# Reordering the head of a Strassen attention-and-MLP kernel: load order of x and w_in, one clamp on VectorE, score order, one transpose group moved

## The chip, the cores and the metric

One core of a Trainium2 chip. The metric is the device time of one execution in microseconds, the median of several runs. The engines are TensorE (PE, with its weight loads PEld), VectorE (DVE), ScalarE (ACT), GpSimd (POOL) and SyncE (SP), which here only issues DMAs.

## The reference

```python
# x (8, 8, 512, 64), state (8, 8, 32, 64), w_in (512, 2048), w_out (2048, 512)
def _attn_ref(x, state):
    scores = scale * np.matmul(x, state.transpose(0, 1, 3, 2))
    a = softmax(scores)                       # exp(s - max) / (sum + 1e-9)
    xread = np.matmul(a, state)
    scores2 = scale * np.matmul(state, x.transpose(0, 1, 3, 2))
    a2 = softmax(scores2)
    sread = np.matmul(a2, x)
    return np.concatenate([xread, sread], axis=2)

def _moe_ref(x, w_in, w_out):                 # x: attention's output as 4352 rows of 512
    h = x @ w_in
    g = h * (1.0 / (1.0 + np.exp(-1.702 * h)))
    return g @ w_out
```
In the kernel w_in and w_out arrive as float64 (two 32-bit words a value) and are turned into float32 on the chip. `softmax` is written out in the original.

## The kernel before, in words

Eight batches go one after the other through attention, the up product with w_in, a gelu, and the down product with w_out. The order of all instructions is written out by hand (`tc.manual_schedule()`): each engine works through its own queue in the order of the program text. The two matrices are multiplied together with the attention first: instead of `(a @ state) @ w_in`, a small matrix M = state @ w_in is made for each quarter of w_in (`att_M`), and the up product is `a @ M`. Down products, and the up products from batch 2 on, use Strassen's scheme.

What matters here is the head, before the first up product (`up_x(0, 0, ...)`), in which batches 0 and 1 go through attention while the first quarter of w_in is still arriving.

**Loads.** `load_weights(n)` issues the loads of the weight pieces up to piece n (512 KB each: 128 rows of w_in, 512 columns, two words a value; pieces 0 to 3 are the first quarter of w_in, 4 to 7 the second, w_out begins at 16). `load_x(b)` issues x of batch b: four loads of 256 KB for batch 0, two of 512 KB for batch 1. All are issued by SP in this order, eight semaphores in turn: pieces 0 and 1, x of batch 0, piece 2, x of batch 1, pieces 3 to 7.

**A weight piece.** On VectorE `mask(i)` (L221) takes the exponent bits; a clamp moves it to float32's range, in `round_a`: two ACTIVATEs on ScalarE (L232, L233), or for pieces 18 and 19 two tensor_scalars on VectorE (L229, L230). `fraction(i)` (L239), `sign(i)` (L245) and the two steps of `round_b` (L258, L264) on VectorE give the value. `powers_to(n)` does mask and clamp up to piece n; `piece(fill)` finishes the next piece, with `fill()` between its last two steps; `round_to(n)` finishes pieces up to n.

**Attention of a batch in the head.** `two_states` and `xT_part` transpose states and x on TensorE (L330, L356), ScalarE copies the results out of PSUM (L334, L357). `att_scores` multiplies them (L444): 16 matmuls, each on a quarter of the array's columns (j) and a half of its rows (i). `score_copies` copies the scores to SBUF on ScalarE (L363), `scores_back` transposes them again on TensorE (L372). `head_max` (L379) and `head_sub` (L386) on VectorE, `head_exp` (L390) on ScalarE, `head_sum` (L402 to L405) and `head_scale` (L413) on VectorE make the softmax; `head_back` transposes it on TensorE (L422, copied by L423 on ScalarE). `att_M` is L430 (copied by `M_copies`, L566), `up_x` runs L655.

**Order in the head.** For batch 0: states, x, scores, and then batch 1's states and x woven with batch 0's softmax. In the kernel before, `scores_back(1, i, ...)` stands ahead of `att_M(0, 0)` and `head_back(0, g)`; `head_max(1, i, ...)` comes on VectorE right behind `head_scale(0)`; `up_x(0, 0)`, `up_x(0, 1)` and `up_x(0, 2)` follow, and then `head_back(1, g)`.

**The second place.** In the down products of batch 0 (loop over `i` in `range(HF)`, L1539), at i = 0, an early up product of batch 1 (`up_x(1, f_early, ...)`), `att_srT`, the sums of w_out (`pair_sums`) and the next two pieces (`round_to`) stand between the products P2 and P6.

Of the kernel before, what the change touches and what calls it, by code (L numbers as in the profile page):

```python
# [20 lines left out]
def kernel(  # L21
# [124 lines left out]
        for g in range(NG):  # L146
            nc.sync.dma_start(stn[b][:, g], st_v[b, g])

    def load_x(b):
        t = sums[:, 0] if b == 1 else xpool.tile([P, SCH, H, D], FP32, tag="xn", name=f"xn_{b}").rearrange("p c h d -> p (c h d)")  # L150
        xn[b] = t.rearrange("p (h c d) -> p h c d", h=H, c=SCH)
        n = NPR if b else NG
        for i in range(H // n):
            h = slice(n * i, n * (i + 1))
            nc.sync.dma_start(xn[b][:, h].rearrange("p h c d -> p h (c d)"), x_four[b, :, h])

    def load_x_squares(b):
        xsq[b] = xpool.tile([P, NPR, S], FP32, tag="xn", name=f"xsq_{b}")
# [57 lines left out]
    def mask(i):  # L216

        _, hi = words(i)
        sc = low[:, 2 + i % (AHEAD + 1)].bitcast(I32)
        power[i] = sc  # L220
        nc.vector.tensor_scalar(sc, hi, 0x7FF00000, None, ALU.bitwise_and)  # L221

    def round_a(i):

        if i not in power:
            mask(i)
        sc = power[i]
        if i in (NFC * NPR + 2, NFC * NPR + 3):
            nc.vector.tensor_scalar(sc, sc, most, least, ALU.min, ALU.max)  # L229
            nc.vector.tensor_scalar(sc, sc, -least, 8.0, ALU.add, ALU.mult)  # L230
            return
        nc.scalar.activation(out=sc.bitcast(FP32), in_=sc, func=AF.Relu, bias=edge[0], scale=-8.0)  # L232
        nc.scalar.activation(out=sc, in_=sc.bitcast(FP32), func=AF.Relu, bias=edge[1], scale=-1.0)  # L233

    def fraction(i):

        key = PIECES[i]
        dst = w_in[key[1]][:, key[2]] if key[0] == "i" else w_out[:, key[1]]
        nc.vector.tensor_scalar(dst.bitcast(I32), words(i)[1], 0xFFFFF, 0x100000, ALU.bitwise_and, ALU.bitwise_or)  # L239
        begun[i] = dst  # L240
# [32 lines left out]
    def load_weights(upto):  # L273
        while done["load"] < min(upto, len(PIECES)):
            load_weight(done["load"])
            done["load"] += 1

    def powers_to(n):
        while done["a"] < min(n, len(PIECES)):
            load_weights(done["a"] + 1)  # L280
            round_a(done["a"])
            done["a"] += 1
# [15 lines left out]
    def piece(fill):  # L298

        i = done["b"]  # L300
        powers_to(i + 1)
        round_b(i, i + 1, False, fill)
        done["b"] += 1
        refill()
# [20 lines left out]
    def two_states(b, banks):  # L325

        A[b]["turn"] = banks
        A[b]["two"] = [apool.tile([P, P], FP32, tag=f"two{i}", name=f"two{i}_{b}", bufs=2) for i in range(2)]
        for ps, t in zip(banks, two):
            nc.tensor.transpose(ps, t[:, b].rearrange("p u d -> p (u d)"), ident)  # L330

    def state_copies(b):
        for t, ps in zip(A[b]["two"], A[b]["turn"]):
            nc.scalar.copy(t, ps)  # L334
# [10 lines left out]
    def xT_part(b, j, bank=None):  # L345

        if j == 0:
            A[b]["xT"] = apool.tile([P, H, 2, P], FP32, tag="xT", name=f"xT_{b}")
        h = slice(NG * j, NG * (j + 1))
        if bank is None:  # L350
            ps = att_ps([P, NG, 2, P], f"xT_{b}_{j}")
        else:
            ps = bank.rearrange("p (g i q) -> p g i q", g=NG, i=2)
        for g in range(NG):
            for i in range(2):
                nc.tensor.transpose(ps[:, g, i], x_pair(b, NG * j + g, i), ident)  # L356
        nc.scalar.copy(A[b]["xT"][:, h], ps)  # L357
# [8 lines left out]
    def scores_back(b, i, bank):  # L366

        ps = bank.rearrange("p (k g m) -> p k g m", k=2, g=NG)
        for k in range(2):
            for g in range(NG):  # L370
                o = P * (2 * g + k)
                nc.tensor.transpose(ps[:, k, g], A[b]["s"][i][:, o : o + P], ident)  # L372

    def head_max(b, i, banks):
        a = A[b]
        if i == 0:
            a["e1"] = apool.tile([P, SCH, NG, NPR, Ns], FP32, tag="e1", name=f"e1_{b}")
            a["mx"] = apool.tile([P, NG, NB], FP32, tag="mx", name=f"mx_{b}")
        nc.vector.reduce_max(out=a["mx"][:, i], in_=banks[i].rearrange("p (k n) -> p k n", n=Ns), axis=AX.X)  # L379
# [8 lines left out]
    def head_exp(b):  # L388
        t = A[b]["e1"]
        nc.scalar.activation(out=t, in_=t, func=AF.Exp, scale=scale)  # L390
# [41 lines left out]
    def att_scores(b):  # L432
        a = A[b]
        a["s"] = bank_o[:NG] if b < 2 else bank_o[NG:]
        if b > 1:
            by_state(b, a["s"], lambda rows, j: a["xT"][rows, j])
            return

        for g in range(NG):
            for j in range(NPR):  # L440
                st = slice(Ns * j, Ns * (j + 1))
                for i in range(2):
                    rows = slice(D * i, D * (i + 1))
                    nc.tensor.matmul(  # L444
                        a["s"][i][st, 2 * P * g : 2 * P * (g + 1)], state_of(b, NG * j + g, i),
                        a["xT"][rows, NG * j + g], start=True, stop=True,
                    )
# [846 lines left out]

    load_two_states()
    load_weights(2)
    load_x(0)
    load_weights(3)
    load_x(1)
    load_weights(2 * NPR)  # L1300
    nc.scalar.activation(out=one, in_=one, func=AF.Exp)
    keep_warm(14)
    powers_to(1)
    fraction(0)
    powers_to(2)
    piece(lambda: fraction(1))
    held, apart = bank_o[NG:], [psH.tile([P, FC], FP32, tag="h", name=f"apart_{i}") for i in range(2)]
    two_states(0, [bank_o[i][:, :P] for i in range(2)])
    state_copies(0)
    keep_warm(3, held[0])  # L1310
    for j in range(NPR):
        xT_part(0, j, apart[j - 2] if j > 1 else None)
    piece(lambda: mask(2))
    powers_to(3)
    att_scores(0)
    fraction(2)
    score_copies(0)
    two_states(1, [apart[i][:, :P] for i in range(2)])
    state_copies(1)
    xT_part(1, 0)  # L1320
    scores_back(0, 0, held[0])
    piece(None)
    head_max(0, 0, held)
    mask(3)
    head_sub(0, 0, held)
    xT_part(1, 1)
    apart = [psH.tile([P, FC], FP32, tag="h", name=f"apart_{i}") for i in (2, 3)]
    xT_part(1, 2, apart[0])
    xT_part(1, 3, apart[1])
    scores_back(0, 1, held[1])  # L1330
    powers_to(NPR)
    att_scores(1)
    head_max(0, 1, held)
    fraction(3)
    head_sub(0, 1, held)
    score_copies(1)
    head_exp(0)
    apart = [psH.tile([P, FC], FP32, tag="h", name=f"apart_{i}") for i in (4, 5)]
    for i in range(2):
        scores_back(1, i, apart[i])  # L1340
    piece(None)
    att_M(0, 0)
    att_M(1, 0, banks=held, copied=False)
    head_sum(0)
    head_scale(0)
    for g in range(NG):
        head_back(0, g)
    M_copies(1, 0)
    for i in range(2):
        head_max(1, i, apart)  # L1350
# [202 lines left out]
    for i in range(HF):  # L1553
        round_to(nin + 2 * i + 2)
        gelus(len(waiting))
        if i == 3:
            nc.scalar.copy(G[1, f_early // 2][:, f_early % 2], early)
        if i == 0:
            pair(i, "P1")
            att_sread(1)  # L1560
            att_M(1, 2, banks=bank_o[1::2])
            att_sread(0)
            att_M(1, 3, True)
            pair(i, "P2")
            f_early = rest.pop(0)
            early = xn[0].rearrange("p h c d -> p (h c d)")[:, :S]
            up_x(1, f_early, dst=early)
            att_srT(0)
            att_srT(1)
            t_room.append(pieces(apool.tile([P, NG, SCH * P], FP32, tag="eT", name="t_room_1"), 2, 2))  # L1570
            s_rooms.append(four(apool.tile([P, NG, NB * Ns], FP32, tag="e1", name="s4_room")))
            pair_sums(i)
            round_to(nin + 4)
            powers_to(nin + 6)
            pair(i, "P6")
            ps7["P7"], ps7["P3"] = (psH.tile([P, FC], FP32, tag="h", name=f"down_{k}") for k in (7, 3))
            ps7["P4"], up_bank = (att_ps([P, FC], f"down_{k}") for k in (4, "up"))
        else:
            pair_sums(i)
            pair(i, "P1", "P2")  # L1580
        if i == 2:
            G[1, f_early // 2] = free.pop(0)
        if i > 1 and i % 2 == 0:
            up_x(1, rest.pop(0), bank=up_bank, wait=True)
        if i == HF - 1:
            k1 = s_rooms[0][:, :2]
            nc.scalar.copy(k1, ps7["P1"].rearrange("p (r n) -> p r n", r=2))
        late()
        if i > 1 and i % 2:
            up_x(1, rest.pop(0), bank=up_bank if i < HF - 1 else bank_o[0], wait=True)  # L1590
        if i == HF // 2 + 1:
            load_state(2)
            load_x_squares(2)
# [140 lines left out]
```

## Time and profile before

| What | us |
|---|---|
| Median of 3 runs (lowest, highest) | 689.87 (689.04, 690.25) |
| Profiled execution, its own time | 688.99 |
| Its span | 687.2 |
| TensorE busy in the span | 677.6 |
| VectorE busy | 558.0 |
| ScalarE busy | 327.9 |
| First up matmul starts at | 24.01 |
| Granted TensorE clock, mean | 0.998 |

The span runs from the first to the last instruction; 1.79 us of the execution's own time lie around it. A row of a timeline gives start, length, engine, line, operation, result and inputs, shape and count, and in brackets the idle time of the engine ahead of it with what ended that. A row's length is from its start to its confirmed end; the next instruction on VectorE or ScalarE can start some 0.08 us before that end.

### The profile page before, as it was taken

The numbers are of one execution on the slowest core, as the hardware profiler recorded it, in microseconds if no ns is written. First come the engines' busy times: TensorE is split into PE (matmuls) and PEld (weight loads), VectorE is DVE, ScalarE is ACT, GpSimd is POOL, SyncE is SP. The second block draws the span as 40 slices with busy tenths as digits, with TensorE's granted clock in tenths as the row PEclk, the third lists the DMA queues.
The fourth block names the chain that finished last, engine by engine and source line by source line (L and its number), as shares of the span: only waits on it lengthen the run. The fifth ranks groups of instructions, "written<-read, shape, count | busy, mean of one in ns | idle before, by whom it ended". The sixth has DMA issues, their size and how long they took to land.

```text
span 687.2 us, 13616 instructions
## 1 busy us (share of the span) xinstructions
PE 677.6 (99%) x5355; PEld 578.7 (84%) x5355; DVE 558.0 (81%) x1066; ACT 327.9 (48%) x725; POOL 1.5 (0%) x10
## 2 busy tenths in 40 slices
PE   8999999999999999999999999999999999999996
PEld 4443687769989999889988998899988998999995
DVE  6999899999998886988878796888698885986540
ACT  7799744134355533752375335544375237421410
POOL 0000000000000000000000000000000000000000
PEclk9999999999999999999999999999999999999999
DMA  9731245338262764156443745176415640251000
GB/s 318 302 105 49 93 140 147 116 119 270 89 156 78 208 192 113 32 166 190 151 67 112 205 144 113 32 208 192 115 27 170 187 152 1 77 169 47 2 3 29
DMA packets 100159, 87.39 MB, mean 127 GB/s; under 512 B 56576, under 2 KB 79616, under 8 KB 100096
## 3 DMA queue, kind: packets, MB, share of 16 engines
q1 hardware_dynamic: 99552, 86.40, 42.6%
q8 instruction: 42, 0.69, 0.4%
q10 hardware_dynamic: 544, 0.13, 0.1%
q14 instruction: 21, 0.17, 0.1%
HBM read 68.94 MB, written 17.56 MB: 126 GB/s over the span
## 4 chain that ended last, share of the span: by engine, by line
PE 94%; DMA 2%; DVE 2%; ACT 1%; issue 0%; DVEq 0%; ACTq 0%
PE low L802 28%; PE o L1212 15%; PE o L802 15%; PE upx L1212 6%; PE o L1539 4%; PE M L430 4%; PE down L1539 3%; PE o L655 3%; PE h L655 3%; PE o L701 3%; PE upw L1212 2%; PE o L851 2%; PE down_up L655 1%; PE o L430 1%; PE sr L622 1%; PE upx_sr L1212 1%
## 5 line engine op out<-in xcount | busy, mean ns | idle before, releaser
L802 PE MATMUL low<-w_out,g_room 128*128 128x128 f32 x416 | 54.3, 276 | 0.0
L802 PEld LDWEIGHTS low<-w_out,g_room 128*128 128x128 f32 x416 | 50.5, 192 | 4.5 <-issue 4.2
L1212 PE MATMUL o<-ta,M 128*128 128x256 f32 x192 | 49.9, 382 | 0.0
L1212 PE MATMUL upx<-aT,M 128*128 128x256 f32 x192 | 49.4, 380 | 0.0
L802 PE MATMUL low<-low,g_room 128*128 128x128 f32 x336 | 43.3, 275 | 0.0
L1212 PEld LDWEIGHTS o<-ta,M 128*128 128x128 f32 x192 | 35.5, 190 | 6.0 <-ACT g_room L1258 1.6
L802 PEld LDWEIGHTS low<-low,g_room 128*128 128x128 f32 x336 | 40.3, 192 | 0.0
L1212 PEld LDWEIGHTS upx<-aT,M 128*128 128x128 f32 x192 | 36.0, 190 | 4.8
L1218 ACT ACTIVATE g_room<-o 128x512 f32<-128x512 f32 (+1 forms) x56 | 31.4, 560 | 10.7 <-PE o L1212 10.7
L802 PE MATMUL low<-sums,later 128*128 128x128 f32 x272 | 34.9, 275 | 0.0
L566 ACT COPY M<-M 128x512 f32<-128x512 f32 x53 | 27.5, 596 | 15.2 <-PE M L430 15.2
L802 PEld LDWEIGHTS low<-sums,later 128*128 128x128 f32 x272 | 32.7, 192 | 0.1
L858 DVE TENSOR_TENSOR g_room<-g_room 128x512 f32<-128x512 f32 x48 | 31.8, 686 | 0.2
L1212 PE MATMUL o<-ta,ms 128*128 128x256 f32 x120 | 30.8, 379 | 0.0
L232 ACT ACTIVATE low<-low,edge 128x512 f32<-128x512 int32 x30 | 21.8, 726 | 17.6 <-DVE low L221 17.6
L1258 ACT COPY g_room<-o 128x512 f32<-128x512 f32 (+1 forms) x28 | 15.6, 556 | 25.0 <-PE o L1212 25.0
L1218 ACT ACTIVATE g_room<-g_room 128x512 f32<-128x512 f32 (+1 forms) x28 | 16.8, 602 | 20.8 <-DVE g_room L1221 20.8
L1212 PEld LDWEIGHTS o<-ta,ms 128*128 128x128 f32 x120 | 22.8, 190 | 3.1
L1212 PE MATMUL o<-aT,m 128*128 128x256 f32 x96 | 24.6, 379 | 0.0
L802 PEld LDWEIGHTS o<-w_out,g_room 128*128 128x128 f32 x160 | 19.4, 192 | 5.0 <-issue 5.0
L430 PE MATMUL M<-w_in,stT 64*32 64x512 f32 x344 | 23.2, 592 | 0.0
L858 DVE TENSOR_TENSOR g_room<-g_room,later 128x512 f32<-128x512 f32 x35 | 22.8, 685 | 0.0
(321 smaller groups left out, 1640.8 us busy)
## 6 DMA issues: line engine op xcount, KB each, us to landing
low<-low SPq DMA_DIRECT2D x108, 256.0 KB, 2.6
low<-low SPq DMA_DIRECT2D x11, 768.0 KB, 4.5
later<-in_moe_w_out_dram SPq DMA_DIRECT2D x16, 512.0 KB, 3.4
w_out<-in_moe_w_in_dram SPq DMA_DIRECT2D x12, 512.0 KB, 10.0
xsq<-in_x_dram SPq DMA_DIRECT2D x96, 64.0 KB, 2.3
xn<-in_x_dram SPq DMA_DIRECT2D x12, 512.0 KB, 4.2
out_dram<-osb SPq DMA_DIRECT2D x15, 256.0 KB, 2.2
out_dram<-later SPq DMA_DIRECT2D x14, 256.0 KB, 2.2
```

Of the source, the lines that this page charges most:

```text
L232: nc.scalar.activation(out=sc.bitcast(FP32), in_=sc, func=AF.Relu, bias=edge[0], scale=-8.0)
L430: nc.tensor.matmul(ps[g][st], state_of(b, NG * j + g, g), rhs(rows, j), start=True, stop=True)
L566: nc.scalar.copy(A[b]["M", c][:, g], ps)
L655: nc.tensor.matmul(hps, lhs[i], rhs[i], start=(i == 0), stop=(i == n - 1))
L701: nc.tensor.matmul(ps[:, r], lhs[f][:, P * r : P * (r + 1)], rhs[:, f], start=(first and r == 0 and f == 0), stop=(f == HF - 1), skip_grou ...
L802: nc.tensor.matmul(ps, lhs[f], rhs[:, f], start=(first and f == 0), stop=(f == QF - 1), skip_group_check=True)
L851: nc.tensor.matmul(ps[:, r], lhs[f][:, P * r : P * (r + 1)], rhs[:, f], start=(r == 0 and f == 0), stop=(f == HF - 1), skip_group_check=True,)
L858: nc.vector.tensor_tensor(out=out, in0=x0, in1=x1, op=op)
L1212: nc.tensor.matmul(ps[:, k], lhs[i][:, o : o + P], rhs[i], start=(first and k == 0 and i == 0), stop=(i == n - 1), skip_group_check=True,)
L1218: nc.scalar.activation(out=dst, in_=src, func=AF.Gelu_apprx_sigmoid)
L1258: nc.scalar.copy(c12, Y(u))
L1539: nc.tensor.matmul(ps7[name][:, HN * r : HN * (r + 1)], lhs[:, P * r : P * (r + 1)], rhs, start=(i == 0 and r == 0), stop=(i == HF - 1), s ...
```

## The change

Four things are changed. (1) `load_x` takes the parts that it is to load, and the loads are issued as: pieces 0 and 1, three quarters of batch 0's x, piece 2, the last quarter, piece 3, batch 1's x, pieces 4 to 7. (2) Piece 0's clamp is done on VectorE. (3) `att_scores` loops over j outside and g inside; the head from there to the first up product is written in a new order, in which `sign` is drawn ahead, pieces 2 and 3 are masked earlier, both `scores_back(0, i)` stand together, and `scores_back(1, i)` comes after `head_back(0, g)`. (4) In the down products `pair_sums` and `round_to` come ahead of P2.

```diff
-    def load_x(b):
+    def load_x(b, parts=None):
+        if not parts or parts[0] == 0:
+            room_x(b)
+        n = NPR if b else NG
+        for i in parts or range(H // n):
+            h = slice(n * i, n * (i + 1))
+            nc.sync.dma_start(xn[b][:, h].rearrange("p h c d -> p h (c d)"), x_four[b, :, h])
+
+    def room_x(b):
         t = sums[:, 0] if b == 1 else xpool.tile([P, SCH, H, D], FP32, tag="xn", name=f"xn_{b}").rearrange("p c h d -> p (c h d)")
         xn[b] = t.rearrange("p (h c d) -> p h c d", h=H, c=SCH)
-        n = NPR if b else NG
-        for i in range(H // n):
-            h = slice(n * i, n * (i + 1))
-            nc.sync.dma_start(xn[b][:, h].rearrange("p h c d -> p h (c d)"), x_four[b, :, h])
@@
-        if i in (NFC * NPR + 2, NFC * NPR + 3):
+        if i in (0, NFC * NPR + 2, NFC * NPR + 3):
             nc.vector.tensor_scalar(sc, sc, most, least, ALU.min, ALU.max)
             nc.vector.tensor_scalar(sc, sc, -least, 8.0, ALU.add, ALU.mult)
@@
-        for g in range(NG):
-            for j in range(NPR):
+        for j in range(NPR):
+            for g in range(NG):
@@
     load_weights(2)
-    load_x(0)
+    load_x(0, range(NPR - 1))
     load_weights(3)
+    load_x(0, [NPR - 1])
+    load_weights(NPR)
     load_x(1)
     load_weights(2 * NPR)
...
     fraction(0)
+    sign(0)
     powers_to(2)
     piece(lambda: fraction(1))
...
-    for j in range(NPR):
+    for j in range(NPR - 1):
         xT_part(0, j, apart[j - 2] if j > 1 else None)
     piece(lambda: mask(2))
     powers_to(3)
+    xT_part(0, NPR - 1, apart[1])
+    fraction(2)
     att_scores(0)
-    fraction(2)
     score_copies(0)
     two_states(1, [apart[i][:, :P] for i in range(2)])
+    sign(2)
+    piece(lambda: mask(3))
+    fraction(3)
+    powers_to(NPR)
+    xT_part(1, 0)
     state_copies(1)
-    xT_part(1, 0)
-    scores_back(0, 0, held[0])
-    piece(None)
-    head_max(0, 0, held)
-    mask(3)
-    head_sub(0, 0, held)
+    for i in range(2):
+        scores_back(0, i, held[i])
+    for i in range(2):
+        head_max(0, i, held)
+        head_sub(0, i, held)
     xT_part(1, 1)
     apart = [psH.tile([P, FC], FP32, tag="h", name=f"apart_{i}") for i in (2, 3)]
     xT_part(1, 2, apart[0])
+    head_exp(0)
     xT_part(1, 3, apart[1])
-    scores_back(0, 1, held[1])
-    powers_to(NPR)
     att_scores(1)
-    head_max(0, 1, held)
-    fraction(3)
-    head_sub(0, 1, held)
     score_copies(1)
-    head_exp(0)
-    apart = [psH.tile([P, FC], FP32, tag="h", name=f"apart_{i}") for i in (4, 5)]
-    for i in range(2):
-        scores_back(1, i, apart[i])
     piece(None)
     att_M(0, 0)
     att_M(1, 0, banks=held, copied=False)
+    apart = [psH.tile([P, FC], FP32, tag="h", name=f"apart_{i}") for i in (4, 5)]
     head_sum(0)
     head_scale(0)
     for g in range(NG):
         head_back(0, g)
+    for i in range(2):
+        scores_back(1, i, apart[i])
     M_copies(1, 0)
@@
+            t_room.append(pieces(apool.tile([P, NG, SCH * P], FP32, tag="eT", name="t_room_1"), 2, 2))
+            s_rooms.append(four(apool.tile([P, NG, NB * Ns], FP32, tag="e1", name="s4_room")))
+            pair_sums(i)
+            round_to(nin + 4, 1)
             pair(i, "P2")
             f_early = rest.pop(0)
             early = xn[0].rearrange("p h c d -> p (h c d)")[:, :S]
             up_x(1, f_early, dst=early)
             att_srT(0)
             att_srT(1)
-            t_room.append(pieces(apool.tile([P, NG, SCH * P], FP32, tag="eT", name="t_room_1"), 2, 2))
-            s_rooms.append(four(apool.tile([P, NG, NB * Ns], FP32, tag="e1", name="s4_room")))
-            pair_sums(i)
-            round_to(nin + 4)
             powers_to(nin + 6)
```

## The prediction

> **What bounds the kernel now.** I read the page's busy times first, then TensorE's waits over the whole run, then the chain that ended last, and only then the first 40 us engine by engine.
>
> ```profile
> PE 677.6 (99%) x5355; PEld 578.7 (84%) x5355; DVE 558.0 (81%) x1066; ACT 327.9 (48%) x725; POOL 1.5 (0%) x10
> ```
> ```profile
> PE warm L131 <- DVE one L123: 1.2, 1, 1.2
> PE apart L372 <- ACT sums L363: 0.8, 1, 0.8
> PE aT L422 <- DVE e L413: 0.6, 1, 0.6
> PE o L330 <- DMA states<-in_state_dram: 0.6, 1, 0.6
> PE o L372 <- ACT sums L363: 0.2, 1, 0.2
> PE xT L356 <- DMA sums<-in_x_dram: 0.2, 1, 0.2
> ```
> TensorE is busy 99% of the span, and these six waits (us in total, times, longest) are all that the whole run shows. All lie ahead of 24 us. GpSimd (10 instructions) and its queue are untouched by the change. So the program is a head of 24 us followed by 663 us of TensorE without a gap, and whatever delays TensorE once after the head stays in the total. The head itself hangs on VectorE, as the chain shows (start, length, what):
>
> ```profile
> 23.16 0.66 DVE mx L379 x2
> ...
> 24.28 1.29 DVE e L386 x2
> ...
> 25.65 1.06 ACT e L390
> ...
> 29.46 1.15 PE o L422 x8
> ```
> The reader is to see that the chain does not run through the first up product. It runs through batch 1's softmax on VectorE (L379, L386), its exponential on ScalarE (L390), and comes to TensorE only at batch 1's `head_back` (L422). TensorE's own timeline says why:
>
> ```profile
> 18.20 1.14 PE L372 MATMUL apart<-ident,sums 128*128 128x128 f32 x8 [0.80 <-ACT sums L363]
> 22.71 1.23 PE L422 MATMUL aT<-ident,e 128*128 128x128 f32 x8 [0.64 <-DVE e L413]
> 24.01 5.42 PE L655 MATMUL h<-aT,M 128*128 128x512 f32 x12
> 29.44 1.17 PE L422 MATMUL o<-ident,e 128*128 128x128 f32 x8
> ```
> Twelve up matmuls begin at 24.01 and issue in 5.43 us; batch 1's transposes follow at 29.44, the moment both TensorE and the scaled `e` are there (`e` of batch 1 is scaled at 28.60, ends 29.30). An earlier first up product alone gains nothing; batch 1's softmax must come earlier too.
>
> VectorE's idle times in the head are what a new order could win:
>
> ```profile
> 6.60 0.43 DVE L221 TENSOR_SCALAR low<-w_out 128x512 int32<-128x512 int32 x1 [0.71 <-DMA w_out<-in_moe_w_in_dram]
> 11.11 0.43 DVE L221 TENSOR_SCALAR low<-w_out 128x512 int32<-128x512 int32 x1 [0.53 <-DMA w_out<-in_moe_w_in_dram]
> 13.09 0.69 DVE L245 SCALAR_TENSOR_TENSOR low<-w_out,low 128x512 int32<-128x512 int32 x1 [0.61 <-ACT low L233]
> 67.12 0.43 DVE L229 TENSOR_SCALAR low<-low 128x512 int32<-128x512 int32 x1
> 67.58 0.43 DVE L230 TENSOR_SCALAR low<-low 128x512 int32<-128x512 int32 x1
> ```
> Together 1.85 us. The last two lines are the clamp on VectorE as it is done later for other pieces: 0.46 us from start to start.
>
> **What the skill says.** "VectorE: DVE Perf Modes", section "The perf-mode tier table": a one-source fp32 operation in SBUF runs at twice the rate of a two-source one; the trace agrees (0.43 against 0.69 us at 512 columns). "ScalarE: Activation LUTs", section "What ACT_TABLE_LOAD costs": an ACTIVATE with a [128,1] bias costs about 280 ns plus 0.833 ns a column, 0.71 us at 512; the clamp's L232 and L233 take 0.72. "TensorE: Matmul & The Clock Gate", section "The mechanism" of Part 3: matmuls on different tiles of the array overlap, and they end in program order. The trace's records of L444 agree: the matmuls of six or eight tiles start within 0.06 us, and a second one on the same tile starts 0.45 us later (two passes of 0.22).
>
> **The loads.** The landings before are: w_in pieces 0 and 1 at 5.02 and 6.58, x of batch 0 at 7.50, 8.25, 9.00 and 9.71, piece 2 at 11.09, batch 1's halves at 12.60 and 14.05, piece 3 at 15.35, piece 4 at 16.63. So 256 KB cost 0.73 us and 512 KB 1.3 to 1.5. The change permutes these in SP's queue: piece 2 lands at 10.38, the last quarter of x at 11.09, piece 3 at 12.5, batch 1's halves at 13.95 and 15.4; from piece 4 on nothing moves. SP waits nowhere longer: the new fourth x load waits for a semaphore of the states' DMA (5.18, as piece 2 did before), and the rings hold work until then.
>
> **VectorE and ScalarE up to piece 2.** Piece 0's clamp leaves ScalarE (two ACTIVATEs, 1.5 us) and adds two tensor_scalars of 0.46 each, 0.92, to VectorE. They fill the 0.71 idle ahead of 6.60. mask(1) starts at 7.27 instead of 6.60; ScalarE clamps piece 1 from 7.80 to 9.35 (before: 7.06 to 8.55), then has the two state copies (0.35) and three x copies (0.48 each), so piece 2's clamp starts at 11.05 and ends 12.55. Piece 2's sign starts at 12.57 instead of 13.09: **0.52 won**.
>
> **The scores.** The last x copy now stands behind that clamp on ScalarE: 12.45 to 13.03 instead of 10.51 to 11.09. The loop order j outside, g inside puts the two matmuls on the same tile back to back. For the last quarter that is two steps of 0.45 after 13.07, so the scores end at about 14.1, against 12.20. Their copies follow at 14.2 to 15.2 (before 12.96 to 14.01). On TensorE batch 1's first transposes (x landed 13.95, no new wait) stand ahead of `scores_back(0)`, which then starts at 14.9 and 15.4, each 0.65 to its end. `head_max(0, 0)` starts at 15.55 instead of 15.03. Of VectorE's work, mask(3) and fraction(3) now lie before it, 0.34 each, and are won back. Then max, sub, max, sub with the sub directly behind its max (0.71, 0.60, 0.71, 0.60), sign, and the two multiply steps of piece 3 put the sum at 20.1 against 20.02. **The head's gain is gone: +0.1.** On ScalarE `head_exp(0)` now waits for the second sub (18.3) ahead of batch 1's last x copy; behind it queue that copy (to 20.0), the score copies of batch 1 (to 22.3) and those of M (to 23.3), all done before their users below need them, at 23.84 and 24.7.
>
> **Batch 1.** Here is the cost. Its `scores_back` moves from 18.20, where TensorE was idle for 0.80 us, to behind `head_back(0)`. Before, `head_max(1, 0)` followed `head_scale` on VectorE without a gap (22.48, then 23.08). After, it needs: the second scale's end (23.25), 0.15 to the first transpose (22.56 to 22.71 before), 0.44 for four transposes of `head_back`, 0.65 for four of `scores_back`, 0.04 to VectorE, which is 24.53; VectorE idles 1.36 us for it. `head_max(1, 0)` is 24.53 - 23.08 = **1.45 late**, and the subs, the exponential, the sum, the scale and L422 follow it at the same distances: 30.9 instead of 29.44. The first up product starts at 24.7 (eight transposes are ahead of it) and its 5.43 us end at 30.1, so TensorE waits 0.75 us there. From that sum (26.74 before) to piece 7's last step, which ends at 39.48, VectorE has no idle time to give back, and TensorE's L430, which begins at 39.19, uses piece 7; both shift alike, so nothing is recovered. The bank of up product 2 is the one that the first of these subs reads: free at 26.4, wanted at 28.1, no wait.
>
> **The down products.** `pair_sums(0)` and `round_to` move ahead of P2. On VectorE the order stays; on ScalarE one clamp pair goes ahead of the early gelu and the state transposes' copies. It fills a ScalarE idle time of 1.65 us (80.0 to 81.64) and takes away VectorE's 1.92 us wait at 83.97. TensorE waits for nothing there, so I count 0. If the clamp pair ran over, the gelu would come up to 0.3 late (the mask at 80.05 plus two ACTIVATEs), with 1.1 us left until TensorE needs its bank at 83.38, so no loss; a gain is at most the 1.92, if TensorE hung on it somewhere after all. I take 0 and keep -1.92 for a rival.
>
> **Sum.** +1.45 on the profiled execution: 687.2 span, 688.99 its own time (1.79 around it), so 690.4. The three runs' median is 689.87, 0.88 above that execution, so I predict 689.87 + 1.45 = **691.3**. About 0.2%, 1.38 us, is what a measurement can tell from no change; the forecast stands on that edge. My own error is about 0.5: the scores' end (13.7 had they overlapped as before, which puts the sum at 19.8 and the total at +1.1) and the landing of batch 1's x (0.3).
>
> **Rivals.**
> *Not slower.* The early pieces win on VectorE: all three idle times go (1.85), the clamp costs 0.92, so batch 0's scale is 0.93 earlier, and with the wait of 1.36 the change nets to +0.4, 690.3; from a gain of 1.36 on it is not slower at all. For it: the diff brings pieces 2 and 3 1 to 3 us sooner. Against it: ScalarE's queue, not the loads, releases piece 2. Chance 0.21.
> *Faster through the second part.* VectorE's 1.92 us near 82 us matter to TensorE, and the head costs nothing: 688.0. Against it: not one TensorE wait after 24 us. Chance 0.05.
> *More than forecast.* Batch 1's x lands one 512 KB slot later than worked out, and stands ahead of `scores_back(0)` in TensorE's queue, so its whole 1.45 goes through: 692.8. Chance 0.12.
> *Forecast.* Chance 0.62, from +0.9 to +2.0; two thirds of it lie above 1.38.
>
> Slower by over 0.2% is 0.42 + 0.12 = 0.54; within 0.2%, 0.21 + 0.20 = 0.41; faster 0.05. The forecast's own range is 690.8 to 691.9; with the nearer halves of the rivals, 690.0 to 692.4.
>
> **What would show it** in the profile after. Right: VectorE idle for over 1 us before batch 1's first L383 (the new number of L379), released by TensorE; a TensorE wait of some 0.7 us at batch 1's L426; piece 2's L249 near 12.6; no VectorE wait near 82 us. Wrong: L426 of batch 1 at or ahead of 29.44, batch 0's sum well ahead of 20.0, or a new TensorE gap after 40 us.

## The result, and the profile after

The changed kernel takes 690.83 us (median of 22 runs, 690.02 to 692.28) against 689.43 (22 runs, 688.82 to 691.01). The ratio is 1.0019, 95% interval 1.0012 to 1.0025, so +1.3 us with bounds of +0.8 and +1.7. That is slower, and just inside the 0.2% that the prediction took as the bound of what can be told from no change. The profiled execution has a span of 688.5 us (before 687.2) and an own time of 690.84.

The page's first line of busy times:

```profile
PE 676.3 (98%) x5355; PEld 579.5 (84%) x5355; DVE 558.9 (81%) x1068; ACT 326.1 (47%) x723; POOL 1.7 (0%) x10
```
Two instructions have moved from ScalarE to VectorE (the clamp of piece 0), 1068 and 723 against 1066 and 725. TensorE still does 676 us of work in 688. What it waits for (us in total, times, longest):

```profile
PE o L334 <- DMA states<-in_state_dram: 1.4, 1, 1.4
PE apart L360 <- DMA xn<-in_x_dram: 1.4, 1, 1.4
PE warm L131 <- DVE one L123: 1.2, 1, 1.2
PE apart L360 <- ACT two L338: 0.9, 1, 0.9
PE o L426 <- ACT low L237: 0.8, 1, 0.8
...
```
Four lines of this list stand before the first up product, at 24.78 us, and change nothing by themselves. The one that counts is the fifth: 0.8 us at L426 is a hole in TensorE's work after the first twelve up matmuls, and before had no such hole.

The chain of waits between 22 and 42 us leads there (start, length, what; the line numbers here are those of before plus 4):

```profile
24.07 0.45 PE apart L376 x4
...
24.55 1.29 DVE mx L383 x2
25.83 1.21 DVE e L390 x2
...
27.12 1.06 ACT e L394
...
30.92 1.16 PE o L426 x8
```
In the kernel before, batch 1's softmax on VectorE began at 23.08, and nothing stood ahead of it but VectorE's own work. Now four TensorE matmuls of `scores_back(1)` (L376) are the link before it. VectorE's timeline gives the size of the wait in its brackets:

```profile
12.65 0.69 DVE L249 SCALAR_TENSOR_TENSOR low<-w_out,low 128x512 int32<-128x512 int32 x1 [0.60 <-ACT low L237]
15.57 0.69 DVE L383 TENSOR_REDUCE mx<-o 128x16 f32<-128x512 f32 x1 [0.34 <-PE o L376]
20.15 1.21 DVE L406 TENSOR_REDUCE sm<-e 128x32 f32<-128x1024 f32 x1
22.00 1.29 DVE L417 TENSOR_TENSOR e<-e,sm 128x512 f32<-128x512 f32 x2
24.55 1.29 DVE L383 TENSOR_REDUCE mx<-apart 128x16 f32<-128x512 f32 x2 [1.25 <-PE apart L376]
```
In the kernel before, the same two steps stood here:

```profile
20.02 1.21 DVE L402 TENSOR_REDUCE sm<-e 128x32 f32<-128x1024 f32 x1
23.08 1.28 DVE L379 TENSOR_REDUCE mx<-apart 128x16 f32<-128x512 f32 x2
```
And TensorE's timeline shows what follows, with the row of before that answers to its last:

```profile
13.15 1.05 PE L448 MATMUL o<-xT,two 64*32 64x256 f32 x8 [0.23 <-ACT xT L361]
22.84 1.23 PE L426 MATMUL aT<-ident,e 128*128 128x128 f32 x8
23.91 1.04 PE L376 MATMUL apart<-ident,sums 128*128 128x128 f32 x8
24.78 5.32 PE L659 MATMUL h<-aT,M 128*128 128x512 f32 x12
30.91 1.17 PE L426 MATMUL o<-ident,e 128*128 128x128 f32 x8 [0.81 <-ACT low L237]
40.59 1.45 PE L434 MATMUL M<-w_in,two 64*32 64x512 f32 x16
```
```profile
39.12 1.46 PE L430 MATMUL M<-w_in,two 64*32 64x512 f32 x16
```
Batch 0's sum starts at 20.15 (before 20.02), so the new order of the early pieces is nearly level. Then VectorE stands idle for 1.25 us, and everything of batch 1 is 1.47 us late: the first maximum 24.55 instead of 23.08, `head_back` 30.91 instead of 29.44. L434, which begins the next stage, is also 1.47 late (40.59 against 39.12), and the span is 1.3 longer. So what comes after 31 us gives back no more than 0.2. Some 0.10 us of the 1.47 is not the kernel's: the first quarter of x landed at 7.60 here and at 7.50 in the profile before.

One name in this view is to be read with care. The wait at L426 is put down to ScalarE's clamp L237, because that ends at 30.91. L426 waits for two semaphores, and VectorE's first scale ends at 30.76, 0.15 earlier. In the kernel before, batch 0's L422 started 0.15 after its first scale too (22.56 to 22.71), with ScalarE's work done since 22.30. By that measure the scale is the releaser; in any case both engines' work here stands behind the same exponential, and that behind the late maximum.

### The profile page after: what moved, and what is told of

The parts are those of the page before. It is cut to its first block, busy times and chain, and to the rows that moved or that the text cites. A ratio compares the mean times of both kernels' runs of the same rounds, so it can differ in the third digit from the quotient of the medians.

```text
span 688.5 us, 13618 instructions
## 1 busy us (share of the span) xinstructions
PE 676.3 (98%) x5355; PEld 579.5 (84%) x5355; DVE 558.9 (81%) x1068; ACT 326.1 (47%) x723; POOL 1.7 (0%) x10
## 4 chain that ended last, share of the span: by engine, by line
PE 95%; ACT 2%; DMA 2%; DVE 1%; issue 0%; DVEq 0%; ACTq 0%
PE low L806 28%; PE o L1216 15%; PE o L806 15%; PE upx L1216 6%; PE o L1546 4%; PE M L434 4%; PE down L1546 3%; PE o L659 3%; PE h L659 3%; PE o L705 3%; PE upw L1216 2%; PE o L855 2%; PE down_up L659 1%; PE o L434 1%; PE sr L626 1%; PE upx_sr L1216 1%
## 5 line engine op out<-in xcount | busy, mean ns | idle before, releaser
L434 PE MATMUL M<-w_in,stT 64*32 64x512 f32 x344 | 23.2, 592 | 0.0
```

The costliest lines, as they stand in the source:

```text
L434: nc.tensor.matmul(ps[g][st], state_of(b, NG * j + g, g), rhs(rows, j), start=True, stop=True)
```

## Experiments

Ratios are to before, measured together with it. "First max" is the start of batch 1's first `head_max`, "back" that of its `head_back`, in the profiled execution. Profiles of different kernels start their loads a little differently: the first quarter of x lands between 7.32 and 7.81 us (before 7.50), which shifts a whole head. The span of each execution is on record too. What lies around it varies between 1.7 and 3.6 us from execution to execution, more than most of these edits are worth, so the spans tell small differences apart better than the times do.

| Kernel | Median us (runs) | Ratio, 95% interval | Span, median (range) | First max | Back |
|---|---|---|---|---|---|
| before | 689.43 (22) | | 687.2 (686.9 to 687.7) | 23.08 | 29.44 |
| after | 690.83 (22) | 1.0019, 1.0012 to 1.0025 | 688.5 (688.2 to 688.9) | 24.55 | 30.91 |
| b_back_late | 690.92 (13) | 1.0021, 1.0013 to 1.0029 | 688.6 (688.1 to 689.3) | 24.38 | 30.74 |
| a_back_mid | 690.45 (13) | 1.0009, 1.0001 to 1.0018 | 687.7 (687.5 to 688.1) | 23.39 | 30.15 |
| a_loads_old | 691.72 (5) | 1.0032, 1.0019 to 1.0044 | 689.7 (689.3 to 689.7) | 25.44 | 31.80 |
| b_clamp | 688.98 (13) | 0.9995, 0.9987 to 1.0003 | 687.0 (686.8 to 687.2) | 23.10 | 29.45 |
| b_down | 689.10 (13) | 0.9994, 0.9986 to 1.0002 | 687.1 (687.0 to 687.4) | 23.03 | 29.39 |
| a_scores_g | 691.22 (11) | 1.0023, 1.0014 to 1.0032 | 688.5 (688.3 to 690.2) | 26.07 | 32.44 |
| a_mid_clamp2 | 689.80 (13) | 1.0004, 0.9996 to 1.0012 | 687.2 (686.9 to 687.4) | 22.84 | 29.60 |
| a_mid_clamp2_max | 689.38 (13) | 1.0001, 0.9993 to 1.0010 | 687.0 (686.9 to 687.3) | 23.18 | 29.94 |
| best | 688.95 (13) | 0.9994, 0.9986 to 1.0003 | 686.4 (686.1 to 686.7) | 22.77 | 29.31 |
| a_warm | 690.35 (20) | 1.0013, 1.0007 to 1.0020 | 688.55 (688.3 to 688.8) | 24.70 | 31.06 |

The spans of before are those of the 104 executions measured together with the other kernels.

### The suspected cause alone: scores_back(1) late, in the kernel before

```diff
     head_exp(0)
-    apart = [psH.tile(...) for i in (4, 5)]
-    for i in range(2):
-        scores_back(1, i, apart[i])
     piece(None)
...
     for g in range(NG):
         head_back(0, g)
+    apart = [psH.tile(...) for i in (4, 5)]
+    for i in range(2):
+        scores_back(1, i, apart[i])
     M_copies(1, 0)
```


> Kernel before, with batch 1's scores_back (and the two banks it takes) moved behind batch 0's head_back, and nothing else of the change. Theory (this place is the cost): batch 1's first head_max starts near 24.4 us instead of 23.08, VectorE idle about 1.3 us ahead of it, batch 1's head_back near 30.8 instead of 29.44, the time +1.35 us against before (+0.20%). Rivals (the later landing of batch 1's x, or the clamp of piece 0 on VectorE, is the cost): no difference from before, since neither is in this kernel.

VectorE's timeline and TensorE's, one line of each:

```profile
24.38 1.29 DVE L379 TENSOR_REDUCE mx<-apart 128x16 f32<-128x512 f32 x2 [1.25 <-PE apart L372]
```
```profile
30.74 1.17 PE L422 MATMUL o<-ident,e 128*128 128x128 f32 x8 [0.81 <-ACT low L233]
```
Loads, clamp and score order are those of before, and still there are the same 1.25 us on VectorE and the same 0.81 on TensorE as in the changed kernel. `head_back` is 1.30 later than before, and the time goes up by 0.21%. With x landed at 7.51 us, as in before, that 1.30 stands against 1.37 in the changed kernel once its later x is taken off. So this one move accounts for nearly all of the loss; added to it, the other parts come to about zero. The 0.21% is a little too high for the move alone: four of the 13 executions show a lower mean clock (0.995 to 0.996) and spans of 689.0 to 689.3, while the other nine, at 688.1 to 688.8, have a median 1.0 us above that of before.

### The same move taken back in part, in the kernel after

```diff
     head_scale(0)
-    for g in range(NG):
-        head_back(0, g)
     for i in range(2):
         scores_back(1, i, apart[i])
+    for g in range(NG):
+        head_back(0, g)
```


> Kernel after, with batch 1's scores_back ahead of batch 0's head_back (behind att_M), and nothing else. Theory (place of scores_back): head_max of batch 1 follows head_scale without a gap near 23.3 us (after: 24.55), TensorE then reaches batch 1's head_back at about 30.2, so about -0.7 us against after and +0.7 against before. Rivals (loads or clamp are the cost): head_max no earlier than 24, the time as after, +1.3 against before.

VectorE's timeline:

```profile
23.39 1.29 DVE L383 TENSOR_REDUCE mx<-apart 128x16 f32<-128x512 f32 x2 [0.23 <-PE apart L376]
```
TensorE's:

```profile
24.89 5.42 PE L659 MATMUL h<-aT,M 128*128 128x512 f32 x12 [0.24 <-ACT aT L427]
30.15 1.04 PE L426 MATMUL o<-ident,e 128*128 128x128 f32 x8
```
The wait of VectorE shrinks from 1.25 to 0.23 us. `head_back` of batch 1 no longer waits: it starts 5.26 us after the first up product, so TensorE's own queue sets it now. `scores_back(1)` simply stands ahead of the first up product, where in before it filled an idle time. About half of the loss is back: +0.6 us on before by the ratio (expected +0.7, interval +0.1 to +1.2). The rivals gave no change from after. The two intervals of the times overlap, but all 13 spans (687.5 to 688.1) lie under all 22 of after (688.2 to 688.9), and the first maximum comes at 23.39 where the rivals had it no earlier than 24, so they are out.

This also shows that the parts don't simply add up. The old place ahead of `att_M` is no longer free in the new order, as batch 1's scores are copied later (ScalarE's timeline, before and after):

```profile
17.58 1.05 ACT L363 COPY sums<-o 128x512 f32<-128x512 f32 x2
```
```profile
21.22 1.07 ACT L367 COPY sums<-o 128x512 f32<-128x512 f32 x2 [1.14 <-PE o L448]
```
`scores_back(1)` needs these copies, which end at 22.29, and M's first matmul runs from 20.26. By these times, an estimate that no run tests, the old place would have held M up by some 2 us.

### The loads of before, in the kernel after

```diff
-    load_x(0, range(NPR - 1))
+    load_x(0)
     load_weights(3)
-    load_x(0, [NPR - 1])
-    load_weights(NPR)
     load_x(1)
```


> Kernel after with the order of loads of before (all of batch 0's x, piece 2, batch 1's x, piece 3). Theory: piece 3 lands at 15.35 instead of 12.4 but its steps now stand ahead of batch 0's softmax on VectorE, so the first head_max comes about 1 us later than in after and everything behind it too: batch 1's head_back near 32.0, +1.05 us on after, about +2.4 on before. Rival (batch 1's later x is what costs): up to 1.4 us faster than after, as fast as before.

VectorE's timeline:

```profile
15.19 0.43 DVE L225 TENSOR_SCALAR low<-w_out 128x512 int32<-128x512 int32 x1 [1.01 <-DMA w_out<-in_moe_w_in_dram]
```
The mask of piece 3, drawn forward in the new order, waits 1.01 us for a piece that now lands behind batch 1's x. `head_back` of batch 1 comes at 31.80, 0.89 later than in after (expected 1.05), and the time is +2.2 us on before by the ratio (expected +2.4). The rival, that batch 1's later x is the cost, asked for a kernel faster than after. The first quarter of x landed 0.28 us earlier here than in after, so the delay proper is 1.17. The new loads are no loss; the new order needs them.

### The clamp alone, and the down products alone, in the kernel before

```diff
-        if i in (NFC * NPR + 2, NFC * NPR + 3):
+        if i in (0, NFC * NPR + 2, NFC * NPR + 3):
```


> Kernel before with piece 0's clamp on VectorE alone. Theory: the two steps (0.92 us) lie in VectorE's idle 0.71 us ahead of piece 1 and in its wait for piece 2 at 11.1, so nothing behind 11.1 us moves later, time within 0.1 us of before; VectorE's wait ahead of piece 2's sign stays or shrinks. Rival (the clamp costs its own time on VectorE): +0.9 us.

Piece 0's two steps run at 5.52 and 5.98 in VectorE's former idle time; mask(1) starts at 6.66 (6.60 before), and VectorE waits for piece 2 at 11.13, as before at 11.11. `head_back` of batch 1 is at 29.45. The ratio's interval holds 1 (-0.9 to +0.2 us); a cost of 0.9 us (0.13%) lies outside it.

```diff
+            pair_sums(i)
+            round_to(nin + 4, 1)
             pair(i, "P2")
...
-            pair_sums(i)
-            round_to(nin + 4)
             powers_to(nin + 6)
```


> Kernel before with the second part of the change alone (pair_sums and round_to for piece 1 ahead of P2). Theory: VectorE's 1.92 us wait near 84 us goes, TensorE waits for nothing there in either kernel, so the time is that of before within 0.2 us. Rival (TensorE hung on that wait): up to -1.9 us.

VectorE's waits between 60 and 100 us are this one in before (us in total, times, longest) and none here or in after:

```profile
DVE low L245 <- ACT low L233: 1.9, 1, 1.9
```
The time does not follow: 0.9994, with an interval from -1.0 to +0.1 us. The gain of 1.9 us that a rival gave is excluded; a VectorE wait that no TensorE instruction stands behind was worth nothing measurable.

### The order of the scores

```diff
-        for j in range(NPR):
-            for g in range(NG):
+        for g in range(NG):
+            for j in range(NPR):
```


> Kernel after with the loops of the scores the other way round (column group outside, quarter of x inside). The prediction's step (two steps on the same tile behind the last copy cost 0.45 us): scores end near 13.75 instead of 14.20, batch 0's sum some 0.3 us earlier, time -0.25 to -0.35 us against after. Rival (TensorE takes its matmuls in program order, so the last copy holds up the second group either way): scores end near 14.2, time as after.

The rival had it right, but a second effect hid it at first. One line of TensorE's timeline, and the granted clock by windows (window, length, TensorE busy with its instructions, granted clock, DMA share, GB/s):

```profile
13.16 1.92 PE L448 MATMUL o<-xT,two 64*32 64x256 f32 x20 [0.76 <-ACT xT L361]
```
```profile
10.00:11.00 1.00, 0.00 (x0) 1.00 1.05 393
11.00:12.00 1.00, 0.81 (x12) 1.00 1.03 374
12.00:13.00 1.00, 0.40 (x12) 1.00 1.10 353
13.00:14.00 1.00, 0.84 (x16) 0.57 1.10 349
14.00:15.00 1.00, 1.00 (x12) 0.50 1.13 394
```
First, the order. With the column group outside, the last quarter's matmuls of group 0 stop the queue until ScalarE's copy is there, and 20 of the 32 matmul records stand behind it instead of 8 (each of the 16 matmuls is two passes). Second, the clock: it falls to half from 13 us, the 64x256 matmuls take 0.63 us instead of 0.38, the scores end at 15.08, and `head_back` of batch 1 at 32.44. A second profile was taken of the same kernel.

> The version with the scores' loops the other way round, profiled a second time. Where TensorE's clock stays at full speed in the head, the matmuls behind the last x copy take 0.38 us each instead of 0.63, the scores end near 14.2 to 14.3 us, and the span is that of after, 688.5 us, within 0.2; where it does not, the span is near 690.0 again.

The clock fell again, with 0.51 from 13 to 14 us and the same span of 690.0. The spans of the 11 timed executions separate the two effects. Four, the profiled one among them, are at 689.9 to 690.2, with the lowest mean clocks (0.997); the other seven are at 688.3 to 688.7, where after's lie (688.2 to 688.9). So the turned loops cost nothing where the clock does not fall, and the fall costs some 1.5 us. That the three long ones without a profile had the fall, and the seven short ones had not, is read from span and mean clock alone. The kernel before has its loops in this order too and bears it out: there 20 matmuls stood behind the last copy, and at full clock they took 1.06 us (11.14 to 12.20), as long as the 8 of after (1.05). By that the scores would end near 14.2 here, an estimate. The j-outside order is therefore neither a gain nor a loss in itself.

### Taking the clamp off ScalarE's queue as well

In the version with `scores_back(1)` ahead of `head_back(0)`:

```diff
-        if i in (0, NFC * NPR + 2, NFC * NPR + 3):
+        if i in (0, 2, NFC * NPR + 2, NFC * NPR + 3):
```


> Kernel after with batch 1's scores_back ahead of batch 0's head_back and piece 2's clamp on VectorE, so that batch 0's last x copy on ScalarE has no clamp ahead of it. Theory (ScalarE's queue makes the scores late): last x copy starts at about 11.6 to 12.0 instead of 12.53, scores end 0.5 to 0.7 earlier, batch 0's first head_max some 0.2 to 0.5 earlier than in after, sum near 19.9, first up product near 24.1, time about +0.1 us against before. Rival (the clamp adds its 0.92 us on VectorE): +0.3 to +0.9 on the version with scores_back moved alone.

The last x copy runs from 11.71 instead of 12.53, the scores are done by 13.43, when their copies start, the sum is at 19.67, and the first maximum of batch 1 at 22.84, 0.24 ahead of before (0.13 of it is x, which landed earlier here). TensorE's timeline:

```profile
24.35 5.42 PE L659 MATMUL h<-aT,M 128*128 128x512 f32 x12 [0.24 <-ACT aT L427]
29.60 1.04 PE L426 MATMUL o<-ident,e 128*128 128x128 f32 x8
```
VectorE is earlier, yet the first up product is 0.34 later than in before (24.35, where 24.1 was expected): its matmuls wait for ScalarE's copies of the transposes. The time can't be told from that of before (-0.3 to +0.8 us). That ScalarE's queue makes the scores late is confirmed; the 0.92 us of the clamp on VectorE lay in the waits that it removed.

The order max, max, sub, sub on top of that:

```diff
     for i in range(2):
         head_max(0, i, held)
+    for i in range(2):
         head_sub(0, i, held)
```


> The version with scores_back moved and piece 2's clamp on VectorE, with batch 0's softmax in the order max, max, sub, sub of the kernel before. Theory: each sub no longer stands directly behind the max that it needs (0.1 us each), sum near 19.7, batch 1's head_back near 29.2, time 0.2 to 0.3 us under before. Rival (TensorE's second bank of scores comes too late for the second max): no difference to the version without it.

Here x landed 0.44 us later than in the profile above. Corrected for it, the sum is 0.22 earlier, as two stalls of 0.11 should give, but batch 1's `head_back` only 0.10: TensorE sets it. The expected 29.2 was 29.94, 29.50 after the correction. The time (1.0001) can't be told from that of the version without it.

### A version from what was learned

It keeps the parts that cost nothing and the early place of `scores_back(1)`:

```diff
-    load_weights(3)
+    load_weights(NPR)
     load_x(1)
...
+    mask(3)
+    fraction(3)
     state_copies(1)
-    xT_part(1, 0)
-    scores_back(0, 0, held[0])
+    for i in range(2):
+        scores_back(0, i, held[i])
     piece(None)
-    head_max(0, 0, held)
-    mask(3)
-    head_sub(0, 0, held)
+    for i in range(2):
+        head_max(0, i, held)
+    for i in range(2):
+        head_sub(0, i, held)
+    powers_to(NPR)
+    xT_part(1, 0)
     xT_part(1, 1)
...
+    head_exp(0)
     att_scores(1)
...
```


> Kernel before, with the parts of the change that cost nothing (piece 0's clamp on VectorE, pair_sums ahead of P2, piece 3 loaded ahead of batch 1's x) and an order of its own: mask and fraction of piece 3 stand in VectorE's wait for piece 2's clamp, both scores_back of batch 0 stand ahead of batch 1's transposes in TensorE's queue, batch 0's softmax is max, max, sub, sub, and batch 1's scores_back stays ahead of att_M and head_back. Theory (VectorE's chain to batch 1's head_back sets the end): the two fillers (0.34 us each) no longer stand between the maxima and the subs, so sum near 19.35 instead of 20.02, first up near 23.4, batch 1's head_back near 28.8 instead of 29.44, about -0.65 us against before (-0.09%). Rival (the later x of batch 1 makes its scores late): head_max of batch 1 waits for TensorE and the gain is gone, 0 to +0.5.

TensorE's timeline:

```profile
24.06 5.42 PE L655 MATMUL h<-aT,M 128*128 128x512 f32 x12 [0.22 <-ACT aT L423]
29.31 1.04 PE L422 MATMUL o<-ident,e 128*128 128x128 f32 x8
```
In this profile x landed 0.30 us later than in before. The sum is at 19.70, so 0.62 earlier once that is taken off, but `head_back` of batch 1, at 29.31, is only 0.43 earlier by the same reckoning: TensorE's row from the scores of batch 1 to the first up product has become the longer chain. The median is 688.95, the lowest of all kernels here, but the interval of the ratio holds 1, so that it beats before is not shown in the time; that it beats after is, since the two intervals do not meet. In the span it is shown: its 13 executions (686.1 to 686.7) all lie below the 32 of before measured with it (686.9 to 687.5), by 0.8 us in the median, where 0.65 was expected.

### TensorE kept at work, and after once more

Four small matmuls in TensorE's idle time ahead of batch 0's last transposes:

```diff
         xT_part(0, j, apart[j - 2] if j > 1 else None)
+    keep_warm(4, held[0])
     piece(lambda: mask(2))
```


> Kernel after with four more keep_warm matmuls in TensorE's idle time ahead of batch 0's last transposes (9.9 to 11.1 us in after). Theory that TensorE's clock falls to half for some us of the head in part of the executions, because TensorE has little to do there: the upper part of after's times (691 to 692.3) goes, the lowest stay near 690.0, the median falls by about 0.5 us. Rival (the spread has another cause): times as after, 690.0 to 692.3 with a median near 690.8.

The times are 690.04 to 690.55 in 20 runs (after: 690.02 to 692.28 in 22, in an earlier measurement), the median 690.35. The lowest stays and the upper part goes, as expected, but the reason given was wrong. After's spans reach only from 688.2 to 688.9 us in 22 executions, with nothing like the 1.5 us that half clock cost in the turned loops, and a_warm's are the same (688.3 to 688.8). What differs lies outside the span: time less span is 1.74 to 3.58 us in after and 1.74 to 1.89 in a_warm. Against before it is +0.9 us by the ratio, an interval that overlaps after's; the hole at L426 is still there in its trace, 0.81 us, as is VectorE's 1.25.

> Kernel after, profiled a second time. If its time lies above 691 us, the granted clock should be near half for some us between 10 and 22 us of the span, and L426 of batch 1 later than 30.91; if it lies near 690.0 to 690.8, the trace should be that of the first profile within 0.1 us.

Its time was 690.89, the clock stayed at 1.00 through the head, and the trace is that of the first profile (L426 of batch 1 at 30.77, with x landed 0.18 earlier). So no profile shows half clock in the head but those of the kernel with the scores turned round. Two executions of after with the clock at full, 690.84 and 690.89, lie above all of a_warm's. What makes the part of after's times outside the span spread stays open, and so does why it did not spread in a_warm's 20 executions; that the four matmuls are the cause is not shown.

## Why the prediction was right

The mechanism was right and so was the size of it. All four signs that it named are there: VectorE idle for 1.25 us before batch 1's first L383, a TensorE wait of 0.81 us at L426, L249 at 12.65, and no VectorE wait near 82 us. The predicted time was less close: 690.83 lies only just inside the forecast's own range, at its lower end.

- **What bounds the kernel.** Read from three views together: TensorE has no gaps after the head, and the chain into it runs through batch 1's softmax on VectorE. The experiment with the one move alone shows it. A delay of batch 1's softmax of 1.30 us became +0.21%, 1.45 us (1.0 us in the spans of the nine executions at the usual clock).
- **Loads.** Piece 2 landed at 10.37, the last quarter at 11.12, piece 3 at 12.41, batch 1's halves at 13.91 and 15.40; the prediction had 10.38, 11.09, 12.5, 13.95 and 15.4.
- **VectorE and ScalarE up to piece 2.** The sign of piece 2 came at 12.65 against a predicted 12.57, so 0.44 won instead of 0.52.
- **Scores.** Their end, 14.20 against 14.1, was right, but one reason given for it was wrong. The text charged 0.45 us to the loop order, for two steps on one tile back to back, and gave 13.7 "had they overlapped as before". But the last x copy feeds both column groups of its quarter, so both steps on that tile stand behind it in either order. The last 8 matmuls took 1.05 us after the copy; in before 20 stood behind it, and took 1.06 (11.14 to 12.20). The whole 2.00 us between 12.20 and 14.20 are the last x copy, which ends at 13.10 instead of 11.09. The turned loops were expected to give 0.3 back and gave nothing. By the Trainium skill, "TensorE: Matmul & The Clock Gate", Part 3, section "The mechanism", matmuls start in program order, so a waiting one holds all behind it. The 20 matmuls that start only after 13.16 in the turned version agree, but twelve of them on other tiles run beside the rest and add no time.
- **Batch 0's sum**, 20.15 against 20.1, and **batch 1**: maximum at 24.55 (24.53), the first up product at 24.78 (24.7), `head_back` at 30.91 (30.9), TensorE's wait 0.81 (0.75). VectorE's idle time was 1.25, not 1.36. Two small errors meet here: with x landed 0.10 later than in before, the delay proper is 1.37 rather than 1.45, so the hundredths agree in part by luck.
- **Down products**, counted as 0: confirmed by the part alone, with VectorE's wait gone and the time the same.
- **The sum.** +1.45 was predicted on the profiled execution; the trace has +1.47 at batch 1's `head_back` and +1.3 in the span. The times have +1.3 by the ratio and +1.40 by the medians. The predicted time, 691.3, is 0.47 too high, and the mis-sized term is the base: the median of three runs, 689.87, stood 0.44 above the 689.43 that 22 runs give. The profiled execution with its 688.99 stood 0.44 below it. Between the two bases the text took the higher and named the gap. One citation is loose: 0.43 against 0.69 us is a ratio of 1.6, not 2. Nothing rests on it, since the sums use the measured steps.

The rival "Not slower" let the gain of the early pieces reach batch 0's scale. It did not, since the scores were late by ScalarE's copy and the head's gain of 0.44 us was spent by 15.57, where VectorE waits 0.34 for TensorE. Piece 2's sign still waited 0.60 us for ScalarE's clamp, as the text held against this rival.

## What to carry to other kernels

When a step is moved, ask what its old place cost. `scores_back(1)` stood in an idle time of TensorE and was free; behind `head_back(0)` it was a link of the chain between two engines, and VectorE waits 1.25 us for it. Ask too whether the old place is still free under the new order of the rest; here, by the times of the copies, it was not, and moving it ahead of `head_back(0)` gave only half of the loss back. A large idle time (1.9 us on VectorE near 82 us) that no later instruction of the bounding engine depends on is worth nothing, and a base taken from three runs can be off by a third of the effect that is being forecast. Where the time around the span varies by more than the effect, compare the spans of all executions: here they told best from before and turned loops from a fallen clock, where the medians could not.

## What the runs showed of the hardware

TensorE's granted clock fell to half for some 3 us in the head of one kernel, in part of its executions. In both profiles of the kernel with turned loops it was 0.50 to 0.57 from 13 to 16 us, after three windows of 1 us in which TensorE was busy for 0.00, 0.81 and 0.40 us (second profile: 0.00, 0.66 and 0.55). In after the same windows hold 0.00, 0.74 and 0.92 (0.00, 0.91 and 0.75), and the clock stayed at 1.00 in both profiles. The Trainium skill, "TensorE: Matmul & The Clock Gate", Part 1, section "What's actually happening", describes this: a monitor that halves the clock after an idle window of some 3.4 us, the windows running freely. The trace agrees that the clock halves, but no idle time there was that long: the longest was about 1.3 us, ahead of the last transposes.

What sets the fall off is not shown. After had an idle time as long (1.38 us) and kept its clock, and in the profile of b_back_late TensorE stood idle for 2.28 us ahead of 20.12 with the clock at 1.00. Seven of the 11 timed executions of the turned kernel have spans without the fall, so the same program can go either way. The price can be read from those spans: 689.9 to 690.2 us with the fall and 688.3 to 688.7 without, some 1.5 us, which is also the distance of `head_back` of batch 1 (32.44 against 30.91 in after). These runs show no share of the loop order in it.
